# Splits of q, k, v at the front of odd slots, low parts on VectorE, and two PSUM banks by turns in a fused attention and two-layer feed-forward kernel

## The chip, the cores and the metric

One core of one Trainium2 chip. The time of a run is the device time in microseconds (us); lower is better. It is given as the median of several runs of the same program.

## The reference

Three stages, each fed by the one before, all in float32:

```python
def _attn_ref(q, k, v):                       # (8, 8, 576, 64) each, chunks of 64
    scores = scale * np.matmul(q_c, k_c.transpose(0, 1, 2, 4, 3))
    scores = scores - np.max(scores, axis=-1, keepdims=True)
    attn = np.exp(scores)
    attn = attn / (np.sum(attn, axis=-1, keepdims=True) + 1e-09)
    out = np.matmul(attn, v_c)
def _moe_ref(x, w_in, w_out):                 # 4608 x 512, 512 x 2048, 2048 x 512
    h = x @ w_in
    g = np.where(h > 0.0, h, np.exp(np.minimum(h, 0.0)) - 1.0)
    return g @ w_out
def _moe2_ref(x, w_gate, w_val, w_out):       # 512 x 1536, 1536 x 512
    return (1 / (1 + np.exp(-(x @ w_gate))) * (x @ w_val)) @ w_out
```

Attention is within chunks of 64 rows, so each head of each chunk is a small independent problem. The weights come as float64.

## The kernel before, in words

**Numbers in parts.** A float32 product is made of rounded parts. `split` (L94) writes the rounded (high) part of a tile as float32r, and a subtraction gives the rest (the low part). The products of the layers then take three passes, high by high, low by high, high by low (`PASSES`, L33). Scores and values of the later pairs use the parts too.

**Phase A and its slots.** The 4608 tokens form nine blocks of 512. For each block, layer 1 (512 to 2048) and layer 2 (2048 to 512) go over 16 strips of 128 hidden columns. One strip of one block is a slot `s`, and `slot` (L431) is an order written out by hand: scheduling is manual, so each engine takes its instructions in the order of the code, with waits where data or buffers ask for them. `layer_1(s)` makes 12 matmuls of 512 columns into a tile `h` (two buffers), `layer_2(s - 2)` makes 12 more into four tiles `y`. Between them ScalarE makes exp and relu (`elu_exp` L378, `elu_rest` L383), VectorE joins them one slot later (`elu_sum`, L386), and `elu_split` (L391) makes the high part on ScalarE and the low part on GpSimd.

**Attention inside the slots.** While block j goes through the layers, the attention of block j + 1 is made, one pair of groups for each two slots, 64 pairs in all. In an even slot pair `P` gets its scores (L243) and its softmax (`softmax_max` L281, `softmax_exp` L296, `softmax_sum` L299). In the next odd slot, pair `T` (the same one) is transposed (L306) and copied out of PSUM by ScalarE (`transposes_out`, L314). In the odd slot after that the pair, now called `V`, is multiplied by v (`values`, L337) and copied to the tile of x of the next block (`values_out`, L364). Pair `N` is the next one to be scored.

**Two kinds of pairs.** The first ten pairs of the slots (`P < P32`) use plain float32 matmuls. They fall in the first 20 slots. Before them `first_block` (L503) makes the attention of block 0. From pair 10 on, `split_qkv` (L230) makes high and low parts of q and v in one tile (`qv`: two ScalarE copies of 64 partitions, two VectorE subtractions) and of k in another (`kz`: a VectorE copy, a GpSimd subtraction). It stands late in the odd slot, after `transposes`. For these pairs `transposes_out` copies twice and issues two small DMAs (`tt`), which mirror the halves of the partitions, and `transposes_split` (L327) opens the next even slot with the high part of the probabilities on VectorE and the low part on GpSimd. `first_parts` (L275) lets ScalarE copy one half of a product out of PSUM, and VectorE adds the other (L292, L371).

**PSUM.** All of attention's matmuls in the slots use one tile of two banks, taken anew for each use (L209, L210); the pool has one buffer, so each new user waits until the last reader of the user before is done:

```python
            def ps_tile(name):
                return ps_a.tile([128, 2, 512], F32, tag="a", name=name)
```

**Other queues.** While slots 0 to 15 run, the weights of layers 1 and 2 are still being converted from float64: `convert` (L106) puts steps for ScalarE and VectorE into a list, and `bg(q[i])` takes some of them at four places in each slot. From slot 16 on to the end of attention that list is empty. In the last slot of a block `split_x` (L174) makes the parts of three chunks of the next block's x, and in the first slot of the next block the fourth; `y_out` (L419) copies the finished y out in the second and third slot, on ScalarE and VectorE by turns. SP issues all loads and stores in the order of the code; `load_raw(P + 1)` opens an even slot.

**Phase B.** After the last block of phase A come the gated layers 3 and 4. Attention plays no part in them.

Of the kernel before, what the change touches and what calls it, by code (L numbers as in the profile page):

```python
# [52 lines left out]
def kernel(  # L53
# [141 lines left out]
    def phase_a():  # L195
        with (
# [12 lines left out]
            def ps_tile(name):  # L209
                return ps_a.tile([128, 2, 512], F32, tag="a", name=name)  # L210
# [18 lines left out]

            def split_qkv(P):  # L230

                r = raws.pop(P)
                k = kz[P] = s_p[0].tile([128, 2, 2, 256], F32R, tag="kz", name="kz")
                t = qv[P] = s_p[0].tile([128, 2, 2, 256], F32R, tag="qv", name="qv", bufs=3)
                h0, h1 = halves
                nc.scalar.copy(out=t[h0, :, 0], in_=r[h0, :, 0:256])
                nc.scalar.copy(out=t[h1, :, 1], in_=r[h1, :, 0:256])
                nc.vector.tensor_copy(out=k[:, :, 0], in_=r[:, :, 256:512])  # L238
                nc.vector.tensor_sub(out=t[h1, :, 0], in0=r[h0, :, 0:256], in1=t[h0, :, 0])
                nc.vector.tensor_sub(out=t[h0, :, 1], in0=r[h1, :, 0:256], in1=t[h1, :, 1])  # L240
                nc.gpsimd.tensor_sub(out=k[:, :, 1], in0=r[:, :, 256:512], in1=k[:, :, 0])  # L241

            def scores(P):  # L243
                ps = st[P, "s"] = ps_tile("ps_s")
                if P < P32:
                    r = raws.pop(P)
                    for i in range(2):
                        for a in range(2):
                            nc.tensor.matmul(
                                out=ps[:, 0, (2 * i + a) * CH:(2 * i + a + 1) * CH],  # L250
                                lhsT=r[:, i, a * 128:(a + 1) * 128],
                                rhs=r[:, i, 256 + a * CH:256 + (a + 1) * CH],
                                start=True,
                                stop=True,
                            )
# [3 lines left out]
                k = kz.pop(P)  # L259
# [21 lines left out]
            def softmax_max(P):  # L281
# [3 lines left out]
                if P < P32:  # L285
                    ps = ps[:, 0, 0:256].rearrange("p (n k) -> p n k", n=4)
# [19 lines left out]
            def transposes(P):  # L306
                ps, p = ps_tile("ps_t"), st.pop((P, "p"))
                st[P, "tp"] = ps[:, 0, 0:256]
                for i in range(2):
                    nc.tensor.transpose(  # L310
                        ps[:, 0, 128 * i:128 * i + 128], p[:, 2 * i:2 * i + 2].rearrange("p n k -> p (n k)"), ident,
# [15 lines left out]
            def transposes_split(P):  # L327
# [6 lines left out]
                    nc.vector, nc.gpsimd,  # L334
                )

            def values(P):  # L337
                ps, t = ps_tile("ps_v"), st.pop((P, "t"))
                st[P, "v"] = ps
                if P < P32:  # L340
                    r = vals.pop(P)
                    for i in range(2):
                        for u in range(2):
                            nc.tensor.matmul(
                                out=ps[:, 0, 128 * i + u * CH:128 * i + (u + 1) * CH],
# [6 lines left out]
                    return  # L352
                for i in range(2):
# [10 lines left out]
            def values_out(P):  # L364
                ps, (x, o) = st.pop((P, "v")), place(P)
                if P < P32:
                    nc.scalar.copy(out=x[:, o:o + 256], in_=ps[:, 0, 0:256])
# [63 lines left out]
            def slot(s, steps=0):  # L431
# [12 lines left out]
                if even:  # L444
                    if is_pair(P + 1, P32):
                        load_raw(P + 1)
                    if is_pair(P - 1, P32):
                        transposes_split(P - 1)
# [17 lines left out]
                if not even and is_pair(V, P32):  # L466
                    values_out(V)
# [15 lines left out]
                if not even:  # L483
                    if is_pair(T):
                        transposes(T)
                    if is_pair(N, P32):
                        split_qkv(N)
                elu_exp(s)
                if even and is_pair(P):
                    softmax_sum(P)  # L490
                bg(q[2])
                if not even and is_pair(T):
                    transposes_out(T)
# [9 lines left out]
            def first_block(load_w):  # L503
# [28 lines left out]
                for k in range(len(pairs) + 5):  # L532
# [22 lines left out]
                    if (n := at(k - 4)) is not None:  # L555
                        ps = ps_v[n] = ps_tile("ps_v")[:, 0].rearrange("p (n u q) -> p n u q", n=4, u=2)
# [235 lines left out]
```

## Time and profile before

| | us |
|---|---|
| median of 3 runs | 1839.76 |
| lowest and highest run | 1838.08 and 1840.18 |
| profiled execution, its own time | 1839.62 |
| span of the profiled execution | 1837.8 |

| engine | share of the span busy |
|---|---|
| TensorE, matmuls | 98% |
| TensorE, weight loads | 81% |
| VectorE | 55% |
| ScalarE | 39% |
| GpSimd | 22% |

The span runs from the first to the last instruction; the rest of the execution's time lies around it. Times in the profile are counted from the start of the span. The engines are named PE (TensorE matmul), PEld (its weight loads), DVE (VectorE), ACT (ScalarE), POOL (GpSimd) and SP (the queue that issues DMAs). A row such as "a L92" is an instruction made at line 92 of the kernel that writes tile a; a line can be that of a helper, so tiles tell more. The ends of matmuls are modelled, so two matmuls that overlap in a row are one behind the other in truth.

### The profile page before, as it was taken

How to read it: one execution, taken by the hardware profiler on the slowest of the kernel's cores; microseconds unless marked ns; L12 is line 12 of the kernel's file. 1: busy time of each engine (PE TensorE's matmuls, PEld its weight loads, DVE VectorE, ACT ScalarE, POOL GpSimd, SP SyncE). 2: the span in 40 equal slices, each digit the busy share in tenths (PEclk: the TensorE clock that was granted, in tenths of full speed). 3: DMA queues.
4: the chain of work that ended last, by engine and by line, in shares of the span. 5: the costliest groups of instructions: out<-in, count | busy, mean ns of one | idle time of the engine just before them, and what ended most of it. 6: DMA issues, size and time to landing. Idle time of an engine off the chain costs nothing.

```text
span 1837.8 us, 21982 instructions
## 1 busy us (share of the span) xinstructions
PE 1798.4 (98%) x8176; PEld 1481.8 (81%) x8176; DVE 1014.6 (55%) x1671; ACT 724.9 (39%) x1411; POOL 412.8 (22%) x305
## 2 busy tenths in 40 slices
PE   7899999999999999999999999999999999999999
PEld 5778878788787878788888888888888888888887
DVE  6887887787888788876758622223222223132222
ACT  6666665566656566666754301111010101010100
POOL 2223454444444454543220000000000000000000
PEclk9899999999999999999999999999999999999999
DMA  6552121121212221212443100001010101010000
GB/s 215 179 170 94 48 76 53 54 81 46 78 58 66 58 72 53 75 60 82 157 121 122 61 18 23 24 1 46 1 46 1 46 1 46 0 47 0 24 1 23
DMA packets 49498, 111.52 MB, mean 61 GB/s; under 512 B 5872, under 2 KB 17904, under 8 KB 49392
## 3 DMA queue, kind: packets, MB, share of 16 engines
q1 hardware_dynamic: 49392, 110.12, 19.0%
q8 instruction: 65, 1.06, 0.2%
q14 instruction: 41, 0.34, 0.1%
HBM read 84.15 MB, written 18.87 MB: 56 GB/s over the span
## 4 chain that ended last, share of the span: by engine, by line
PE 83%; DVE 8%; ACT 5%; issue 2%; DMA 1%; SPq 0%; DVEq 0%; ACTq 0%
PE o L668 16%; PE pg L181 16%; PE pv L181 16%; PE h L181 16%; PE y L411 15%; PE ps_s L262 1%; DVE qv L240 1%; DVE kz L238 1%; PE ps_v L355 1%; DVE elu L387 1%; DMA tt<-tt 1%; DVE s L294 1%; ACT xs L90 1%; ACT elu L384 1%; DVE t L146 1%
## 5 line engine op out<-in xcount | busy, mean ns | idle before, releaser
L181 PE MATMUL h<-xs,w 128*128 128x512 f32 x1728 | 426.0, 395 | 1.3 <-DVE xs L96 1.3
L411 PE MATMUL y<-g,w 128*128 128x512 f32 x1728 | 424.0, 394 | 0.6 <-DVE y L428 0.6
L657 DVE TENSOR_TENSOR sg<-pv,sg 128x512 f32<-128x512 f32 x108 | 74.6, 691 | 549.8 <-PE pv L181 543.0
L411 PEld LDWEIGHTS y<-g,w 128*128 128x128 f32 x1728 | 319.7, 188 | 66.0 <-DVE y L428 1.0
L181 PEld LDWEIGHTS h<-xs,w 128*128 128x128 f32 x1728 | 317.8, 189 | 64.2 <-DVE xs L96 3.8
L652 ACT ACTIVATE sg<-pg 128x512 f32<-128x512 f32 x108 | 64.4, 597 | 673.5 <-PE pg L181 673.5
L181 PE MATMUL pg<-xs,w 128*128 128x512 f32 x1296 | 311.3, 389 | 0.0
L181 PE MATMUL pv<-xs,w 128*128 128x512 f32 x1296 | 311.3, 389 | 0.0
L668 PE MATMUL o<-w,g 128*128 128x512 f32 x1296 | 311.1, 389 | 0.0
L181 PEld LDWEIGHTS pv<-xs,w 128*128 128x128 f32 x1296 | 243.2, 188 | 50.5
L181 PEld LDWEIGHTS pg<-xs,w 128*128 128x128 f32 x1296 | 243.2, 188 | 50.5
L668 PEld LDWEIGHTS o<-w,g 128*128 128x128 f32 x1296 | 243.2, 188 | 50.5
L96 POOL TENSOR_TENSOR g<-elu,g 128x512 fp32r<-128x512 f32 x144 | 198.7, 1380 | 362.8 <-ACT g L90 353.9
L96 POOL TENSOR_TENSOR xs<-xr,xs 128x512 fp32r<-128x512 f32 x29 | 40.9, 1409 | 814.3 <-ACT xs L90 814.1
L387 DVE SCALAR_TENSOR_TENSOR elu<-h,elu 128x512 f32<-128x512 f32 x144 | 99.5, 691 | 44.6 <-ACT elu L384 42.9
L90 ACT CAST g<-elu 128x512 fp32r<-128x512 f32 x144 | 89.1, 618 | 51.3 <-DVE elu L387 50.4
L241 POOL TENSOR_TENSOR kz<-raw,kz 128x512 fp32r<-128x512 f32 x54 | 96.5, 1787 | 19.1 <-DVE kz L238 16.6
L381 ACT ACTIVATE elu<-h 128x512 f32<-128x512 f32 x144 | 86.0, 597 | 23.0 <-PE h L181 16.6
L96 POOL TENSOR_TENSOR pt<-tt,pt 128x512 fp32r<-128x512 f32 x54 | 70.0, 1297 | 104.9 <-DVE pt L92 98.6
L384 ACT ACTIVATE elu<-elu 128x512 f32<-128x512 f32 x144 | 91.0, 632 | 3.5
L240 DVE TENSOR_TENSOR qv<-raw,qv 64x512 fp32r<-64x512 f32 x54 | 90.3, 1672 | 1.7
L90 ACT CAST w<-t 128x512 fp32r<-128x512 f32 x68 | 42.2, 621 | 95.0 <-DVE t L146 93.8
(74 smaller groups left out, 1465.9 us busy)
## 6 DMA issues: line engine op xcount, KB each, us to landing
raw<-in_qkv SPq DMA_DIRECT2D x54, 512.0 KB, 3.6
wraw<-in_w_out SPq DMA_DIRECT2D x28, 512.0 KB, 3.6
xr<-ymid SPq DMA_DIRECT2D x36, 256.0 KB, 3.6
wraw<-in_w_in SPq DMA_DIRECT2D x16, 512.0 KB, 3.7
ymid<-y SPq DMA_DIRECT2D x32, 256.0 KB, 2.8
out<-o SPq DMA_DIRECT2D x32, 256.0 KB, 2.0
tt<-tt SPq DMA_DIRECT2D x108, 64.0 KB, 2.0
wraw<-in_w_gate SPq DMA_DIRECT2D x12, 512.0 KB, 3.5
```

The costliest lines, as they stand in the source:

```text
L90: nc.scalar.copy(out=out, in_=raw)
L96: lo_eng.tensor_sub(out=lo, in0=raw, in1=hi)
L181: nc.tensor.matmul(out=ps, lhsT=w[:, zw, kk * 128:(kk + 1) * 128], rhs=xs[key, kk][:, zx], start=(kk == 0 and n == 0), stop=(kk == KC - 1 ...
L240: nc.vector.tensor_sub(out=t[h0, :, 1], in0=r[h1, :, 0:256], in1=t[h1, :, 1])
L241: nc.gpsimd.tensor_sub(out=k[:, :, 1], in0=r[:, :, 256:512], in1=k[:, :, 0])
L381: nc.scalar.activation(out=e_t[s], in_=h_t[s], func=ACTF.Exp)
L384: nc.scalar.activation(out=e_t[s], in_=e_t[s], func=ACTF.Relu, scale=-1.0, bias=1.0)
L387: nc.vector.scalar_tensor_tensor(out=e_t[s], in0=h_t.pop(s), scalar=0.0, in1=e_t[s], op0=ALU.max, op1=ALU.subtract,)
L411: nc.tensor.matmul(out=y_t[j, e], lhsT=w[:, zw, e * 128:(e + 1) * 128], rhs=g[:, zx], start=(f == 0 and n == 0), stop=(f == F1 - 1 and n = ...
L652: nc.scalar.activation(out=sg, in_=pg, func=ACTF.Sigmoid)
L657: nc.vector.tensor_tensor(out=sg, in0=pv, in1=sg, op=ALU.mult)
L668: nc.tensor.matmul(out=o_t[t], lhsT=g[:, zx, t * 128:(t + 1) * 128], rhs=w[:, zw], start=(f == 0 and n == 0), stop=(f == F2 - 1 and n == 2),)
```

## The change

It has four parts.

- `split_qkv` is moved from behind `transposes` to the front of the odd slot, behind `elu_sum`. The high part of k becomes a function of its own, `split_k`, which stands before `values_out`; the rest stands behind `values_out`.
- The low part of k and the low part of the probabilities go from GpSimd to VectorE. `transposes_split` moves from the front of the even slot to behind `softmax_max`.
- The two banks are one tile for the whole phase. Plain float32 products and the transposes take one bank each, by turns (`bank`); the products of the later pairs take both.
- `transposes_out` stands right behind `elu_exp`, ahead of the third place of background steps.

```diff
--- before.py
+++ after.py
@@ -206,8 +206,14 @@
             s_p = [None]
             halves = (slice(0, 64), slice(64, 128))
 
-            def ps_tile(name):
-                return ps_a.tile([128, 2, 512], F32, tag="a", name=name)
+
+            banks = ps_a.tile([128, 2, 512], F32, name="banks")
+            turns = [0]
+
+            def bank(n):
+                turns[0] ^= 1
+                return banks[:, turns[0], 0:n]
+
 
             def load_raw(P):
                 if P < P32:
@@ -227,27 +233,29 @@
                 hp, c = divmod(i, 2)
                 return xr_tile(j + 1, hp), 256 * c
 
+
+            def split_k(P):
+                k = kz[P] = s_p[0].tile([128, 2, 2, 256], F32R, tag="kz", name="kz")
+                nc.vector.tensor_copy(out=k[:, :, 0], in_=raws[P][:, :, 256:512])
+
             def split_qkv(P):
-
-                r = raws.pop(P)
-                k = kz[P] = s_p[0].tile([128, 2, 2, 256], F32R, tag="kz", name="kz")
+                r, k = raws.pop(P), kz[P]
                 t = qv[P] = s_p[0].tile([128, 2, 2, 256], F32R, tag="qv", name="qv", bufs=3)
                 h0, h1 = halves
                 nc.scalar.copy(out=t[h0, :, 0], in_=r[h0, :, 0:256])
                 nc.scalar.copy(out=t[h1, :, 1], in_=r[h1, :, 0:256])
-                nc.vector.tensor_copy(out=k[:, :, 0], in_=r[:, :, 256:512])
+                nc.vector.tensor_sub(out=k[:, :, 1], in0=r[:, :, 256:512], in1=k[:, :, 0])
                 nc.vector.tensor_sub(out=t[h1, :, 0], in0=r[h0, :, 0:256], in1=t[h0, :, 0])
                 nc.vector.tensor_sub(out=t[h0, :, 1], in0=r[h1, :, 0:256], in1=t[h1, :, 1])
-                nc.gpsimd.tensor_sub(out=k[:, :, 1], in0=r[:, :, 256:512], in1=k[:, :, 0])
 
             def scores(P):
-                ps = st[P, "s"] = ps_tile("ps_s")
                 if P < P32:
-                    r = raws.pop(P)
+                    ps, r = bank(256), raws.pop(P)
+                    st[P, "s"] = ps
                     for i in range(2):
                         for a in range(2):
                             nc.tensor.matmul(
-                                out=ps[:, 0, (2 * i + a) * CH:(2 * i + a + 1) * CH],
+                                out=ps[:, (2 * i + a) * CH:(2 * i + a + 1) * CH],
                                 lhsT=r[:, i, a * 128:(a + 1) * 128],
                                 rhs=r[:, i, 256 + a * CH:256 + (a + 1) * CH],
                                 start=True,
@@ -256,7 +264,8 @@
                     if P + 1 < P32:
                         load_raw(P + 1)
                     return
-                k = kz.pop(P)
+                ps, k = banks, kz.pop(P)
+                st[P, "s"] = ps
                 for i in range(2):
                     for u in range(2):
                         nc.tensor.matmul(
@@ -283,7 +292,7 @@
                 m = a_p.tile([128, 4, 1], F32, tag="m", name="m")
                 ps = st.pop((P, "s"))
                 if P < P32:
-                    ps = ps[:, 0, 0:256].rearrange("p (n k) -> p n k", n=4)
+                    ps = ps.rearrange("p (n k) -> p n k", n=4)
                     nc.vector.tensor_reduce(out=m[:, :, 0], in_=ps, op=ALU.max, axis=AX.X)
                     nc.vector.tensor_tensor(out=s, in0=ps, in1=m.to_broadcast([128, 4, CH]), op=ALU.subtract)
                     return
@@ -304,11 +313,11 @@
                 nc.vector.tensor_tensor(out=p, in0=e4[:, :, 0:CH], in1=d.to_broadcast([128, 4, CH]), op=ALU.mult)
 
             def transposes(P):
-                ps, p = ps_tile("ps_t"), st.pop((P, "p"))
-                st[P, "tp"] = ps[:, 0, 0:256]
+                ps, p = bank(256), st.pop((P, "p"))
+                st[P, "tp"] = ps
                 for i in range(2):
                     nc.tensor.transpose(
-                        ps[:, 0, 128 * i:128 * i + 128], p[:, 2 * i:2 * i + 2].rearrange("p n k -> p (n k)"), ident,
+                        ps[:, 128 * i:128 * i + 128], p[:, 2 * i:2 * i + 2].rearrange("p n k -> p (n k)"), ident,
                     )
 
             def transposes_out(P):
@@ -331,18 +340,18 @@
                     tt.rearrange("p u i q -> p (u i) q"),
                     t[:, :, :, 0].rearrange("p u i q -> p (u i) q"),
                     t[:, :, :, 1].rearrange("p u i q -> p (u i) q"),
-                    nc.vector, nc.gpsimd,
+                    nc.vector, nc.vector,
                 )
 
             def values(P):
-                ps, t = ps_tile("ps_v"), st.pop((P, "t"))
-                st[P, "v"] = ps
+                t = st.pop((P, "t"))
                 if P < P32:
-                    r = vals.pop(P)
+                    ps, r = bank(256), vals.pop(P)
+                    st[P, "v"] = ps
                     for i in range(2):
                         for u in range(2):
                             nc.tensor.matmul(
-                                out=ps[:, 0, 128 * i + u * CH:128 * i + (u + 1) * CH],
+                                out=ps[:, 128 * i + u * CH:128 * i + (u + 1) * CH],
                                 lhsT=r[:, i, u * 128:(u + 1) * 128],
                                 rhs=t[:, 128 * i + u * CH:128 * i + (u + 1) * CH],
                                 start=True,
@@ -350,6 +359,7 @@
                             )
                     load_values(P + 1)
                     return
+                ps = st[P, "v"] = banks
                 for i in range(2):
                     for u in range(2):
                         nc.tensor.matmul(
@@ -364,7 +374,7 @@
             def values_out(P):
                 ps, (x, o) = st.pop((P, "v")), place(P)
                 if P < P32:
-                    nc.scalar.copy(out=x[:, o:o + 256], in_=ps[:, 0, 0:256])
+                    nc.scalar.copy(out=x[:, o:o + 256], in_=ps)
                     return
                 x1 = st.pop((P, "v1"))
                 for a, p in enumerate(halves):
@@ -444,8 +454,6 @@
                 if even:
                     if is_pair(P + 1, P32):
                         load_raw(P + 1)
-                    if is_pair(P - 1, P32):
-                        transposes_split(P - 1)
                     if is_pair(P):
                         scores(P)
                     if is_pair(P, P32):
@@ -463,8 +471,15 @@
                     elu_sum(s - 1)
                 if even and is_pair(P):
                     softmax_max(P)
-                if not even and is_pair(V, P32):
-                    values_out(V)
+                if even and is_pair(P - 1, P32):
+                    transposes_split(P - 1)
+                if not even:
+                    if is_pair(N, P32):
+                        split_k(N)
+                    if is_pair(V, P32):
+                        values_out(V)
+                    if is_pair(N, P32):
+                        split_qkv(N)
                 bg(q[0])
                 if s >= EARLY:
                     layer_1(s, 2)
@@ -480,17 +495,14 @@
                     softmax_exp(P)
                 if last:
                     split_x(nxt, 1, nc.vector)
-                if not even:
-                    if is_pair(T):
-                        transposes(T)
-                    if is_pair(N, P32):
-                        split_qkv(N)
+                if not even and is_pair(T):
+                    transposes(T)
                 elu_exp(s)
+                if not even and is_pair(T):
+                    transposes_out(T)
                 if even and is_pair(P):
                     softmax_sum(P)
                 bg(q[2])
-                if not even and is_pair(T):
-                    transposes_out(T)
                 elu_rest(s)
                 if last:
                     split_x(nxt, 2, nc.gpsimd)
@@ -553,7 +565,7 @@
                                 ps[:, i], work[n][2][:, 2 * i:2 * i + 2].rearrange("p v k -> p (v k)"), ident,
                             )
                     if (n := at(k - 4)) is not None:
-                        ps = ps_v[n] = ps_tile("ps_v")[:, 0].rearrange("p (n u q) -> p n u q", n=4, u=2)
+                        ps = ps_v[n] = bank(512).rearrange("p (n u q) -> p n u q", n=4, u=2)
                         for i in range(2):
                             nc.tensor.matmul(
                                 out=ps[:, 2 * i:2 * i + 2].rearrange("p v a q -> p (v a q)"),
```

## Rows read from the trace of the kernel before

**Rows 1.** The page: busy time by engine, and one group of instructions

```profile
PE 1798.4 (98%) x8176; PEld 1481.8 (81%) x8176; DVE 1014.6 (55%) x1671; ACT 724.9 (39%) x1411; POOL 412.8 (22%) x305
...
L90 ACT CAST g<-elu 128x512 fp32r<-128x512 f32 x144 | 89.1, 618 | 51.3 <-DVE elu L387 50.4
```

**Rows 2.** Stretches: busy us and count by engine, granted TensorE clock, DMA share, GB/s

```profile
40.00:150.00 110.00, 97.38 (x471) 79.70 (x469) 91.44 (x188) 77.05 (x150) 24.44 (x14) 0.94 0.52 161
...
250.00:860.00 610.00, 598.07 (x2801) 487.87 (x2800) 484.17 (x738) 372.70 (x758) 294.03 (x206) 1.00 0.21 62
860.00:1838.00 978.00, 974.04 (x4298) 806.20 (x4296) 337.32 (x570) 189.62 (x325) 38.22 (x28) 1.00 0.13 41
```

**Rows 3.** Waits of 44 to 157 us: total us, times, longest

```profile
ACT w L90 <- DVE t L146: 33.0, 21, 2.9
PE ps_s L249 <- ACT t L319: 12.0, 7, 3.8
...
DVE m L287 <- PE ps_s L249: 1.8, 3, 0.8
```

**Rows 4.** Timeline at 54 us: start, us, instruction, [idle before <-releaser]

```profile
54.58 1.97 PE L249 MATMUL ps_s<-raw 128*128 128x64 f32 x8 [3.83 <-ACT t L319]
```

**Rows 5.** Timeline of one pair of slots inside a block

```profile
611.12 0.63 PE L262 MATMUL ps_s<-kz,qv 128*128 128x256 f32 x4
...
611.59 2.90 PE L181 MATMUL h<-xs,w 128*128 128x512 f32 x12
611.79 0.75 ACT L279 COPY s<-ps_s 64x256 f32<-64x256 f32 x2 [1.57 <-PE ps_s L262]
611.87 0.43 DVE L92 CAST pt<-tt 128x512 fp32r<-128x512 f32 x1 [0.82 <-DMA tt<-tt]
...
612.43 1.30 POOL L96 TENSOR_TENSOR pt<-tt,pt 128x512 fp32r<-128x512 f32 x1 [1.93 <-DVE pt L92]
612.94 0.85 DVE L292 TENSOR_TENSOR s<-ps_s,s 64x256 f32<-64x256 f32 x2
...
613.81 1.29 POOL L96 TENSOR_TENSOR g<-elu,g 128x512 fp32r<-128x512 f32 x1
613.82 0.42 DVE L293 TENSOR_REDUCE m<-s 128x4 f32<-128x256 f32 x1
...
614.27 1.10 DVE L294 TENSOR_TENSOR s<-s,m 128x256 f32<-128x256 f32 x1
...
617.05 0.63 PE L355 MATMUL ps_v<-pt,qv 128*128 128x256 f32 x4
...
619.39 1.38 DVE L238 CAST kz<-raw 128x512 fp32r<-128x512 f32 x1
...
620.79 0.69 DVE L239 TENSOR_TENSOR qv<-raw,qv 64x512 fp32r<-64x512 f32 x1
620.84 1.80 POOL L241 TENSOR_TENSOR kz<-raw,kz 128x512 fp32r<-128x512 f32 x1 [0.36 <-DVE kz L238]
...
621.51 1.68 DVE L240 TENSOR_TENSOR qv<-raw,qv 64x512 fp32r<-64x512 f32 x1
...
623.24 0.63 PE L262 MATMUL ps_s<-kz,qv 128*128 128x256 f32 x4
```

**Rows 6.** Waits of 250 to 860 us

```profile
PE ps_s L262 <- POOL kz L241: 7.3, 14, 1.0
```

**Rows 7.** Timeline of TensorE: first scores of the third and of the eighth block

```profile
255.84 0.39 PE L262 MATMUL ps_s<-kz,qv 128*128 128x256 f32 x1 [0.97 <-POOL kz L241]
...
761.15 0.39 PE L262 MATMUL ps_s<-kz,qv 128*128 128x256 f32 x1 [0.97 <-POOL kz L241]
```

**Rows 8.** Timeline of the first and third slot of one block

```profile
461.79 1.22 DVE L96 TENSOR_TENSOR xs<-xr,xs 128x512 fp32r<-128x512 f32 x1 [0.70 <-ACT xs L90]
...
476.69 2.89 PE L411 MATMUL y<-g,w 128*128 128x512 f32 x12
...
477.48 0.69 DVE L428 COPY y<-y 128x512 f32<-128x512 f32 x1 [0.60 <-DMA ymid<-y]
```

## The prediction, made before the changed kernel was run

> **What bounds the kernel now.** I read the page's busy times first, then the stretches, then the waits, then the order of work in one pair of slots. TensorE is busy for 98% of the span [rows 1], so only its waits can be won. Three stretches differ [rows 2]. From 860 us on TensorE is busy for 974.04 of 978 us, a matmul each 0.227 us (978 / 4298), and the change does not touch that code. In 250:860 it loses some 12 of 610 us, in 40:150 some 12.6 of 110. Busy time flatters TensorE, since matmul ends are modelled; below I go by starts.
>
> The first slots lose to one wait: seven times, 12.0 us in all, `scores` waits for ScalarE's copy of the transposes (L319) [rows 3]. Its single PSUM tile is still to be read by that copy: at 54.58 TensorE had sat for 3.83 us [rows 4]. The copy is late because ScalarE stands in the weight conversion: it waits 33.0 us there for VectorE's sums, and VectorE waits only 1.8 us for TensorE's scores [rows 3]. These two set their own pace; TensorE is held to it.
>
> The attention stage has a pair of slots with no wait: scores at 611.12, values at 617.05, next scores at 623.24, a period of 12.12 us [rows 5]. Eight pairs, a block, would be 97.0 us. But from the scores at 255.84 to those at 761.15, five blocks, 505.3 us pass [rows 7], so a block loses 4.1 us against 97.0. Most of it stands at the block's edge, where the splits of x join the queues and `scores` waits for GpSimd's low part of k, 14 times [rows 6]. With the sixth edge the stage loses some 6 x 4.1 = 24.6 us.
>
> **The change, part by part.** Times in this part are after the scores' first matmul of a pair (611.12 is 0, values 5.93, next scores 12.12) [rows 5].
>
> *Low part of k to VectorE.* GpSimd loses 1.80 us a pair. VectorE gains one subtraction of 512 elements: 0.69, as L239 when it runs clear. But L240, the same work beside GpSimd's L241, took 1.68, and the conversion L238 beside GpSimd's low part of g 1.38 [rows 5]; the like conversion L92, clear, took 0.43. So VectorE gives 0.69 and gets back about 1.0 twice. Bounds: 0.69 if clear, 1.68 if held.
>
> *Splits at the front of odd slots.* VectorE now does elu_sum (0.69, taken as L239's, as long), the high part of k (0.43), `values_out`, then three subtractions. I lay it out: values at 5.93, elu_sum to 6.7, high k to 7.1, `values_out` (ScalarE's copies, 0.67 after the values as after the scores, end at 7.35) to 8.2, low k to 8.9, first q to 9.7. ScalarE has put its two q copies (0.62 each, as the high part of g [rows 1]: 7.35 to 8.6) ahead of that high part, so GpSimd's low part of g (1.29) runs 9.7 to 10.9 and holds the last subtraction, which ends at 11.4. The next scores load weights one matmul, 0.23, before 12.12, at 11.9: 0.5 to spare, where before L240 ended (623.19) just under the scores (623.24) [rows 5]. High g comes 1.2 later, but layer 2 wants it only behind the next scores and 12 matmuls of layer 1, at 12.12 + 0.47 + 2.72 = 15.3 (0.47 is from 611.12 to 611.59 [rows 5], 2.72 is 12 x 0.227); free. If that cover went, it would cost those 1.2. No DMA moves but those of `transposes_out`, two per odd slot on SP; it now stands ahead of a background step, of which this stage has none. In the first slots it has no DMA. SP's load of the next k, q, v is released earlier, as the raw tile is read out sooner; nothing.
>
> *Low part of the probabilities to VectorE, after `softmax_max`.* GpSimd loses 1.30 a pair. In even slots VectorE no longer begins with the conversion L92 that waits for a DMA. elu_sum runs before the scores; the two sums L292 (0.85, after the ScalarE copies that end at 1.42) to 2.3, the maximum (0.42) to 2.75; the subtraction L294 is held by GpSimd's g, about 2.1 to 3.4, and ends 0.3 after it, 3.7 (before: 615.37, 0.27 after GpSimd). Then high 0.43 and low 0.69: 4.85. The values load weights at 5.7: 0.85 to spare, so in a pair in the middle of a block nothing is won and nothing lost. `softmax_sum` ends near 5.95, and the transposes want it at about 9.1.
>
> *At a block's edge* the parts collide anew. The splits of k and q end before the scores, by the order above with GpSimd's x parts between, at about -0.5: the wait at the scores goes. But in the first slot VectorE has the low part of x chunk 3 (1.22 held [rows 8], 0.7 clear) and that of chunk 1 ahead of elu_sum, which ends near 3.5. ScalarE's high g (0.62) and GpSimd's 1.29 follow, to 5.55, L294 ends at 5.85, the probabilities at 7.0: the values wait 7.0 - 5.7 = 1.3 us. That is late next. In the slot after, the chain shifts by as much and the last q part ends some 0.2 late. Two slots on, VectorE's copy of y (477.48, 0.69) now follows the two parts of the probabilities, 1.12, where it followed one, 0.43. It ended at 478.17, and TensorE overwrote that tile at 476.69 + 9 x 0.227 = 478.73 [rows 8]: 0.56 to spare, less 0.7 and the shift; I take 0.35. New loss 1.85 a block against 4.1: 2.25 won, six times, **13.5 us**. Bounds: 0 if the edge gives all back, 24.6 if nothing takes its place.
>
> *Two banks by turns.* Scores, values and transposes are three uses a pair, so each finds the other bank than the one before it; scores no longer follow the transposes' copy. At most 12.0 us, plus 0.7 for transposes behind `values_out`. But the pace of VectorE and ScalarE stays: what TensorE wins is lead, until another need holds it: the transposes want the probabilities of the slot before, layer 2 its g. That is most of a slot, 6 to 7 us. VectorE has light slots once conversion ends and can catch up, so the lead is kept. I take **6 us**; bounds 1.8 (only VectorE's wait for TensorE goes) and 12.7.
>
> **Sum.** The profiled execution took 1839.62, within 0.2 of the runs' median 1839.76. 1839.6 - 13.5 - 6 = 1820.
>
> **Rivals.** *The queue of VectorE becomes the bound (slower).* The probabilities are ready 0.85 before the values need them; if VectorE's low part were held by GpSimd once more (1.29), they would be 0.44 late in each of the 54 pairs, 24 us, against 19.5 won: 1844. It decides at 0.36 late a pair. For it: VectorE is busy 484 of 610 us and GpSimd 294 there [rows 2], and work goes to the busier. Against: GpSimd keeps one operation a slot, and that one is already charged. The Trainium skill, "Perfetto Trace Analysis", section "Optimizing Scalar/DVE Operations", speaks for this rival: a saturated VectorE may hand work to GpSimd, and moving work between those two might not help, since they share a read port. By it the two moves would win nothing and only the banks would pay, 1834; the trace shows VectorE held by GpSimd (1.68 against 0.69), which bears out the shared port, but not a saturated VectorE.
>
> *The edge gives everything back.* Waits of the values and of y replace those of the scores in full: 1839.6 - 6 = 1834. For it: the 1.3 above is my least certain step.
>
> *The edge closes wholly and the first slots gain all:* 1839.6 - 24.6 - 12.7 = 1802. Against: VectorE's pace [rows 3].
>
> *The banks do not part.* `banks` is one tile; if a wait covers the tile and not the bank, scores wait as before: 1839.6 - 13.5 = 1826. In the trace nothing shows which.
>
> **How the numbers follow.** Forecast 0.50, edge gives back 0.22, all closes 0.12, banks do not part 0.08, slower 0.08. The range, 1807 to 1835, leaves out the slower case, most of the case where all closes, and ends of the bounds. About 0.2% (3.7 us) is what a measurement of this kernel can tell from no change. Below 1836: nearly all of the forecast, most of the edge case, and the two others, 0.86; within: 0.05; above 1843.5: 0.09.
>
> **What would show it.** The row "scores waits for ScalarE t L319" gone, and TensorE's waits for GpSimd's kz with it; block periods near 98.9 instead of 101; a wait of the values for VectorE's pt, about 1.3 us, once a block; pairs still 12.12; L240's time nearer 0.7 for one of the two q parts. I am wrong if pairs inside a block are longer than 12.12, if scores in the first slots still wait, or if the first slots win 12 us.

## The result, and the profile after

| | median us | runs from ... to |
|---|---|---|
| before | 1839.97 | 1838.08 to 1840.64 |
| changed | 1822.46 | 1821.61 to 1823.99 |

The ratio is 0.9907, with an interval of 0.9890 to 0.9925: 0.9% faster, more than the interval leaves open, and 2.5 us from the 1820 forecast. The profiled execution took 1822.07 us. The two terms of the sum came out unlike their sizes, though, and that their errors nearly cancelled is luck.

The page of the changed kernel: busy time by engine.

```profile
PE 1787.4 (98%) x8176; PEld 1480.7 (81%) x8176; DVE 1012.6 (56%) x1779; ACT 729.6 (40%) x1411; POOL 260.2 (14%) x197
```

GpSimd lost 152.6 us of work against [rows 1], and VectorE, which took it, is busy no longer than before.

The stretches (columns as in [rows 2]):

```profile
40.00:150.00 110.00, 99.13 (x475) 80.78 (x474) 91.92 (x189) 77.19 (x151) 24.50 (x14) 0.94 0.52 161
250.00:860.00 610.00, 604.96 (x2875) 502.18 (x2874) 497.40 (x854) 389.68 (x781) 165.23 (x114) 1.00 0.23 69
```

In 250:860 TensorE went from 598.07 to 604.96 us, in 40:150 only from 97.38 to 99.13. The attention stage itself is read from one header of the timeline of the scores of pairs 10 to 63: start of the first and the last of 216 matmuls, before and after.

```profile
L262 PE MATMUL ps_s<-kz,qv x216: 278/280/388, 169.3 to 837.0; 128*128 128x256 f32 x108
```

```profile
L271 PE MATMUL banks<-kz,qv x216: 278/279/282, 168.5 to 819.4; 128*128 128x256 f32 x108
```

The stage took 667.7 us and takes 650.9: **16.8 us won** there. The first slots gave only 169.3 - 168.5 = **0.8 us**. Together 17.6; the two profiled executions differ by 1839.62 - 1822.07 = 17.55. The 0.8 us show no gain: five kernels below (splits late, low k on GpSimd, both runs on the parts of the probabilities, `elu_sum` first) have the changed kernel's code in the slots up to 15, and in their profiled executions pair 10 starts between 170.0 and 171.5. From the third pair's scores to those of pair 10, 169.33 - 54.58 = 114.75 us passed before and 168.53 - 53.94 = 114.59 after: the first slots won nothing that shows.

The first slots' waits, 44 to 157 us, against [rows 3]:

```profile
ACT w L90 <- DVE t L146: 32.1, 21, 2.5
...
PE banks L257 <- ACT t L328: 9.0, 7, 2.9
DVE d L310 <- ACT e L306: 8.4, 7, 1.7
```

The wait that the banks by turns were to end is still there, seven times: the scores (now L257) wait for ScalarE's copy of the transposes (now L328), which lies in the other bank. TensorE's waits in 165 to 860 us, by contrast, are down to a single kind, six times, once a block (matmuls, then weight loads):

```profile
PE banks L365 <- DVE pt L96: 5.0, 6, 0.9
```

```profile
PEld banks L365 <- DVE pt L96: 7.6, 6, 1.3
```

The first slot of one block after the change, the timeline of 540 to 562 us:

```profile
545.81 1.48 POOL L96 TENSOR_TENSOR xs<-xr,xs 128x512 fp32r<-128x512 f32 x1 [5.93 <-ACT xs L90]
...
546.16 1.67 DVE L249 TENSOR_TENSOR qv<-raw,qv 64x512 fp32r<-64x512 f32 x1
...
548.59 0.63 PE L271 MATMUL banks<-kz,qv 128*128 128x256 f32 x4
...
550.67 0.69 DVE L96 TENSOR_TENSOR xs<-xr,xs 128x512 fp32r<-128x512 f32 x1 [1.13 <-ACT xs L90]
551.40 0.69 DVE L397 SCALAR_TENSOR_TENSOR elu<-h,elu 128x512 f32<-128x512 f32 x1
...
552.87 1.28 POOL L96 TENSOR_TENSOR g<-elu,g 128x512 fp32r<-128x512 f32 x1 [2.17 <-ACT g L90]
...
553.34 1.09 DVE L303 TENSOR_TENSOR s<-s,m 128x256 f32<-128x256 f32 x1
554.36 0.41 DVE L92 CAST pt<-tt 128x512 fp32r<-128x512 f32 x1
554.81 0.69 DVE L96 TENSOR_TENSOR pt<-tt,pt 128x512 fp32r<-128x512 f32 x1
555.55 0.74 PE L365 MATMUL banks<-pt,qv 128*128 128x256 f32 x4 [0.82 <-DVE pt L96]
```

The last part of q ends at 547.83, 0.76 ahead of the scores, which wait for nothing. Then VectorE idles for a part of x with `elu_sum` behind it, and the chain elu_sum, high g, low g on GpSimd, subtraction, parts of the probabilities ends at 555.50, 6.91 after the scores. The values are late by it. The stage's first pair lasts 12.60 us (12.59 before), a block's first pair 13.24 to 13.31, every other 12.12 to 12.16.

### The profile page after: what moved, and what is told of

Its sections match the earlier page's. It is cut to its first block, busy times and chain, and to the rows that moved or that the text cites. A ratio compares the mean times of both kernels' runs of the same rounds, so it can differ in the third digit from the quotient of the medians.

```text
span 1820.3 us, 21691 instructions
## 1 busy us (share of the span) xinstructions
PE 1787.4 (98%) x8176; PEld 1480.7 (81%) x8176; DVE 1012.6 (56%) x1779; ACT 729.6 (40%) x1411; POOL 260.2 (14%) x197
## 4 chain that ended last, share of the span: by engine, by line
PE 91%; DVE 4%; ACT 3%; issue 1%; DMA 0%; SPq 0%; DVEq 0%; ACTq 0%
PE y L421 19%; PE h L181 19%; PE o L680 16%; PE pv L181 16%; PE pg L181 16%; PE banks L365 1%; PE banks L271 1%; PE banks L319 1%; DVE t L146 1%; DVE elu L397 1%; ACT t L124 1%; ACT w L90 1%; DMA qkv<-in_qkv 0%; DVE t L140 0%; ACT g L90 0%
## 5 line engine op out<-in xcount | busy, mean ns | idle before, releaser
L96 POOL TENSOR_TENSOR g<-elu,g 128x512 fp32r<-128x512 f32 x144 | 213.0, 1479 | 606.8 <-ACT g L90 348.9
L288 ACT COPY s<-banks 64x256 f32<-64x256 f32 x216 | 79.1, 366 | 122.9 <-PE banks L271 71.5
L301 DVE TENSOR_TENSOR s<-banks,s 64x256 f32<-64x256 f32 x108 | 45.5, 422 | 62.7 <-ACT s L288 62.0
```

The source lines that it names most:

```text
L96: lo_eng.tensor_sub(out=lo, in0=raw, in1=hi)
L288: nc.scalar.copy(out=t[p], in_=parts_of(st[P, what], p, a)[0])
```

## The experiments

All changes are against the changed kernel unless another is named. "Stage" is the time between the first and the last scores of pairs 10 to 63, read as above (667.7 before, 650.9 changed).

### Turns: one tile, two tiles, and the copy's place

**No turns.** The tile is taken anew for each use, as before, and nobody alternates.

```diff
-            banks = ps_a.tile([128, 2, 512], F32, name="banks")
-            turns = [0]
+            def ps_tile():
+                return ps_a.tile([128, 2, 512], F32, tag="a", name="banks")
             def bank(n):
-                turns[0] ^= 1
-                return banks[:, turns[0], 0:n]
+                return ps_tile()[:, 0, 0:n]
...
```

> The changed kernel without turns: each product takes the one tile of two banks anew, as before the change. Theory 1, the turns never parted anything, since a wait covers the tile: same waits in the first slots, total 1822 within 1.5. Theory 2, the turns are worth something in the first block or where a use needs only one bank: scores' waits for ScalarE's t go from 9.0 back to 12.0 us and the total to 1824 to 1826.

Measured: 1822.75 us, ratio 0.9903 (0.9888 to 0.9918). Its waits of 44 to 157 us:

```profile
PE banks L256 <- ACT t L327: 9.0, 7, 2.9
```

Time and wait are those of the changed kernel, to 0.3 us and to the digit, as theory 1 said. The turns inside one tile part nothing.

**Two tiles.** In slots 0 to 15 the banks are two tiles of one bank each; from slot 16 on one tile of two banks.

```diff
...
             def bank(n):
                 turns[0] ^= 1
-                return banks[:, turns[0], 0:n]
+                return both[0][:, turns[0], 0:n] if s_p[0] else both[turns[0]][:, 0:n]
...
+                both[:] = [ps_1.tile([128, 512], F32, name=f"bank{i}") for i in range(2)]
...
+                s_p[0], both[:] = p2, [ps_a.tile([128, 2, 512], F32, name="banks")]
```

> The changed kernel, with the two banks as two tiles of their own while slots 0 to 15 run (one tile of both banks from slot 16 on, as now). Theory 1, a wait covers the whole tile, not the bank: scores' seven waits for ScalarE's copy of the transposes (9.0 us) and the transposes' four for the copy of the values (2.1) go from TensorE's rows; TensorE wins lead, some 5 to 8 us, total 1815 to 1818. Theory 2, the banks part already and what holds the first slots is the pace of VectorE and ScalarE: the waits get other names, the total stays at 1822 within 2.

Measured: 1821.22 us, ratio 0.9900 (0.9885 to 0.9915). The timeline at slots 14, 16 and 18 (at 136.24, 153.23 and 168.00), first of this kernel, then of the changed one:

```profile
136.24 1.10 PE L255 MATMUL bank<-raw 128*128 128x64 f32 x8
...
153.23 1.10 PE L255 MATMUL banks<-raw 128*128 128x64 f32 x8 [1.78 <-ACT t L326]
154.15 4.59 PE L181 MATMUL h<-xs,w 128*128 128x512 f32 x12
154.77 1.57 DVE L96 TENSOR_TENSOR xs<-xr,xs 128x512 fp32r<-128x512 f32 x1 [1.35 <-ACT xs L90]
...
168.00 0.63 PE L269 MATMUL banks<-kz,qv 128*128 128x256 f32 x4
```

```profile
141.86 1.10 PE L257 MATMUL banks<-raw 128*128 128x64 f32 x8 [0.89 <-ACT t L328]
...
155.52 1.00 PE L257 MATMUL banks<-raw 128*128 128x64 f32 x8
```

The scores wait for the copy no more but once, where the tile of two banks begins (153.23), and at slot 14 TensorE leads by 141.86 - 136.24 = 5.6 us. At slot 16 the lead is 2.3, at slot 18 (168.5 against 168.00) 0.5, less than executions differ by. So two tiles do part the uses, and a lead as large as the forecast's 6 us arises; but it is lost again where the weight conversion ends. There block 1's first layer takes 4.59 instead of some 3.0, as it needs the parts of x, which stand in ScalarE's and VectorE's queues behind the last conversions: one is still in the making at 154.77. The time is therefore that of theory 2, 1822 within 2, though its reason, that the banks parted already, is not so. In 44 to 157 us TensorE's waits have other names: the transposes wait 2.8 us for the probabilities and layer 2 waits 2.6 us for low parts of g, as the prediction said that lead would be held.

**The copy late.** Only `transposes_out` goes back behind the third place of background steps.

```diff
-                if not even and is_pair(T):
-                    transposes_out(T)
                 if even and is_pair(P):
                     softmax_sum(P)
                 bg(q[2])
+                if not even and is_pair(T):
+                    transposes_out(T)
```

> The changed kernel with its copy of the transposes put back behind the third place of background steps. Theory 1 (that place is what shortened the scores' waits for the copy from 12.0 to 9.0 us): the waits of 44 to 157 us are back at 11 to 13 us, the attention stage keeps its 98.2 us a block, 1823.5 to 1826 us. Theory 2 (the copy's early place also matters in the attention stage, where its two DMAs feed the parts of the probabilities): blocks grow beyond 99 us and the time is above 1828.

Measured: 1824.77 us, ratio 0.9917 (0.9903 to 0.9932); the stage as in the changed kernel (170.7 to 821.7, 651.0). The waits of 44 to 157 us:

```profile
PE banks L257 <- ACT t L328: 11.0, 6, 3.9
```

This is as theory 1 said: the copy's place made most of the fall from 12.0 to 9.0. In time it is worth some 2 us, which the intervals do not part from nothing.

### The attention stage: place or engine

**Splits late again**, with all low parts still on VectorE.

```diff
-                if not even:
-                    if is_pair(N, P32):
-                        split_k(N)
-                    if is_pair(V, P32):
-                        values_out(V)
-                    if is_pair(N, P32):
-                        split_qkv(N)
+                if not even and is_pair(V, P32):
+                    values_out(V)
...
                     transposes(T)
+                if not even and is_pair(N, P32):
+                    split_k(N)
+                    split_qkv(N)
                 elu_exp(s)
```

> The changed kernel, with the splits of q, k, v back behind the transposes, low parts still on VectorE. Theory 1 (place): the chain ends 0.9 us after the scores want it at the edge, scores wait there for VectorE's qv, a block loses 2.5 to 3 us where it now loses 1.2, total 1830 to 1834. Theory 2 (engine): the total stays within 3 us of 1822.

Measured: 1842.36 us, ratio 1.0011 (1.0002 to 1.0021): more than the whole gain is gone, and more than was expected to go. The stage took 669.5. TensorE's waits of 165 to 860 us:

```profile
PE banks L271 <- DVE qv L249: 7.7, 6, 1.3
PE banks L271 <- DVE qv L248: 4.0, 6, 0.7
PE banks L365 <- DVE pt L96: 2.6, 3, 0.9
```

The scores wait for the splits again, now for VectorE instead of GpSimd [rows 6]. The splits late with low k on GpSimd, as before the change, were not run, so the 20 us are the price of the late place with low k on VectorE.

**Low k on GpSimd**, at the new place: one word, `nc.vector` to `nc.gpsimd`, in `split_qkv`.

> The changed kernel, with the low part of k back on GpSimd at its new, early place. Theory 1, the place in the queues is what won the edge: pairs inside a block stay at 12.13 and blocks lose at most 0.5 more, total 1822 to 1826. Theory 2, freeing GpSimd is what won it (GpSimd's own 1.8 us and the VectorE subtraction that it holds): scores wait for GpSimd's kz at every edge as before, block periods near 101, total 1835 to 1838.

Measured: 1823.49 us, ratio 0.9912 (0.9897 to 0.9927), no difference from the changed kernel that these intervals show; the stage took 650.8 (170.5 to 821.3). VectorE's groups of 250 to 760 us, in this kernel:

```profile
L249 DVE TENSOR_TENSOR qv<-raw,qv 64x512 fp32r<-64x512 f32 x42 | 39.7, 945 | 1.3
L248 DVE TENSOR_TENSOR qv<-raw,qv 64x512 fp32r<-64x512 f32 x42 | 34.8, 829 | 1.3
```

and in the changed one:

```profile
L249 DVE TENSOR_TENSOR qv<-raw,qv 64x512 fp32r<-64x512 f32 x42 | 70.3, 1674 | 1.3
L247 DVE TENSOR_TENSOR kz<-raw,kz 128x512 fp32r<-128x512 f32 x42 | 29.1, 693 | 1.3
L248 DVE TENSOR_TENSOR qv<-raw,qv 64x512 fp32r<-64x512 f32 x42 | 28.8, 685 | 1.3
```

VectorE spends 0.693 + 0.685 + 1.674 = 3.05 us a pair on the three subtractions, against 0.829 + 0.945 = 1.77 on two: the move costs it 1.28 us a pair, all of it hidden. At the new place k's engine makes no difference that shows, as theory 1 said.

**Parts of the probabilities at the front of the even slot again**, both on VectorE.

```diff
                         load_raw(P + 1)
+                    if is_pair(P - 1, P32):
+                        transposes_split(P - 1)
                     if is_pair(P):
                         scores(P)
...
-                if even and is_pair(P - 1, P32):
-                    transposes_split(P - 1)
```

> The changed kernel, with the parts of the probabilities back at the front of the even slot, both on VectorE. Theory 1, their new place behind softmax_max is what makes the values wait at the edge: that wait (1.1 us a block) goes, but x chunk 3 and elu_sum now stand behind them, so layer 1 waits 0.5 to 1 us there: total 1818 to 1822, pairs inside a block 12.13. Theory 2, VectorE's conversion that waits for the DMA costs in every pair, as everything on VectorE stands behind it: pairs inside a block over 12.2, total 1826 or more.

Measured: 1839.90 us, ratio 0.9997 (0.9987 to 1.0007): the whole gain is gone; the stage took 668.4. VectorE's timeline in a pair inside a block:

```profile
611.68 0.43 DVE L92 CAST pt<-tt 128x512 fp32r<-128x512 f32 x1 [2.12 <-DMA tt<-tt]
...
612.87 0.69 DVE L397 SCALAR_TENSOR_TENSOR elu<-h,elu 128x512 f32<-128x512 f32 x1
```

VectorE stands 2.12 us for the mirroring DMA with `elu_sum` behind it. TensorE's waits of 165 to 860 us show what comes late by that: the transposes, y and the scores.

```profile
PE banks L319 <- ACT qv L246: 5.6, 11, 0.9
PE y L421 <- DVE y L438: 4.2, 4, 1.9
PE banks L271 <- DVE qv L249: 2.7, 4, 0.8
```

The values' wait is gone, as theory 1 said, but the time is on theory 2's side: beside 14.0 to 14.5 us for a block's first pair, several other pairs now take 12.3 to 14.3. The place behind `softmax_max` is therefore as necessary as that of the splits: without either, the whole gain is lost.

**Low part of the probabilities on GpSimd**, at the new place: the last argument of `transposes_split` from `nc.vector` to `nc.gpsimd`.

> The changed kernel, with the low part of the probabilities back on GpSimd at the new place. Theory 1 (VectorE's 0.69 against GpSimd's 1.3): ready 0.65 later, so the values wait 1.75 at the edge instead of 1.1, and pairs inside a block just make it (0.15 to spare): total 1825 to 1828. Theory 2, GpSimd's freedom matters: the low part also holds VectorE's softmax sums and the values wait in every pair, total over 1835.

Measured: 1829.44 us, ratio 0.9938 (0.9923 to 0.9953): 7 us of the gain lost, of which 5.2 in the stage, which took 656.1. TensorE's waits of 165 to 860 us:

```profile
PE banks L365 <- POOL pt L96: 4.8, 6, 0.8
PE banks L319 <- ACT qv L246: 3.5, 6, 0.6
```

The time is 1.4 us above theory 1's range, and the values' wait did not grow as that theory said: 4.8 us against 5.0. The loss stands in the two pairs behind that one, with 12.77 to 12.97 and up to 12.37 us, where the transposes now wait. ScalarE's timeline in the first of them:

```profile
573.91 0.60 ACT L391 ACTIVATE elu<-h 128x512 f32<-128x512 f32 x1 [2.48 <-POOL g L96]
```

GpSimd makes the low part of the probabilities ahead of the low part of g, which so ends later; ScalarE's next exp waits 2.48 us for it (1.45 in the changed kernel), with the copies of the values behind it in the queue. That the transposes come late by this is read from the order, not tested.

Here the engine counts. The Trainium skill, "Perfetto Trace Analysis", section "Optimizing Scalar/DVE Operations", warns that moving work between VectorE and GpSimd might not help, as they share a read port. The trace agrees for k (no change shown) and not for the probabilities (7 us), where another operation stood behind the moved one in GpSimd's queue and ScalarE waited for it.

### The rest of the edge

**`elu_sum` first.** In a block's first slot VectorE waits for a part of x with `elu_sum` behind it (550.67 above). The two change places.

```diff
-                if f == 0 and j > 0:
-                    split_x(j, KC - 1, nc.vector)
                 if s > 0:
                     elu_sum(s - 1)
+                if f == 0 and j > 0:
+                    split_x(j, KC - 1, nc.vector)
```

> The changed kernel, with elu_sum ahead of the low part of x chunk 3 in the first slot of a block (two lines of code change places). Theory 1, the values wait at the edge because VectorE sits idle for ScalarE's chunk 3 with elu_sum queued behind it, and GpSimd's low part of g then holds the softmax subtraction: the wait goes, block periods fall from 98.2 to about 97.1, six or seven times 1.1, total 1815 to 1816. Theory 2, VectorE has simply too much work at the edge: the loss moves to the next scores or to y, block periods stay near 98, total 1821 to 1823.

Measured: 1817.67 us, ratio 0.9880 (0.9865 to 0.9895). The stage took 644.7 (170.9 to 815.6), 6.2 less, some 1.0 for each of six edges. The values' wait is gone, so the chain does begin with the idle time before 550.67. The total is 1.7 us above theory 1's range; pair 10 came at 170.9 in this execution.

**Both**, two tiles and `elu_sum` first.

> Two tiles for the banks in slots 0 to 15 and elu_sum ahead of x chunk 3. The first won 1 us and the second 5. Theory 1, they lie in different stretches and add: 1816 to 1817. Theory 2, TensorE's lead is lost where the parts of x for block 1 are late at slot 16; with elu_sum ahead of chunk 3 that is the place that moves, so more of the lead is kept: 1812 to 1815.

Measured: 1814.83 us, ratio 0.9859 (0.9844 to 0.9873). The stage takes 644.2, and pair 10 starts at 168.2. The time lies in theory 2's range, but its reason is not shown: against the kernel with `elu_sum` first alone (170.9) pair 10 comes 2.7 us earlier, no more than executions differ by, and TensorE's lead over the changed kernel still falls from 5.5 us at slot 14 (136.38) to 0.3.

### What holds the first slots

ScalarE's and VectorE's timelines in that last kernel, with two tiles and `elu_sum` first:

```profile
100.88 0.62 ACT L90 CAST w<-t 128x512 fp32r<-128x512 f32 x1 [2.13 <-DVE t L146]
...
102.47 0.41 ACT L304 ACTIVATE e<-s 128x256 f32<-128x256 f32 x1
```

```profile
100.76 0.42 DVE L137 TENSOR_SCALAR t<-t 128x512 uint32<-128x512 uint32 x1
102.92 0.43 DVE L308 TENSOR_REDUCE d<-e 128x4 f32<-128x260 f32 x1 [1.74 <-ACT e L304]
```

ScalarE's high copy of a converted weight waits 2.13 us for VectorE's sum, and the exponentials stand behind it; then VectorE waits 1.74 us for the exponentials. Each waits for the other in turn. So, in that kernel, the copy is issued later, at the next place of background steps.

```diff
+    high = {}
     def bg(n):
+        for m in list(high):
+            high.pop(m)()
...
             load(n + ahead)
+            high[n] = lambda: make_high(n)
+
+        def make_high(n):
             w = halves[n] = tiles[n][2].tile([128, 2, 512], F32R, tag="w", name="w")
             copy(nc.scalar, w[:, 0], parts[n].bitcast(F32))
         def rest(n):
+            high.pop(n, bool)()
```

> Two tiles and elu_sum first, as in the kernel of 1814.8 us; besides, ScalarE's high copy of a converted weight, which waits for VectorE's sum, is issued at the next place of background steps rather than right behind that sum's issue. Theory 1 (ScalarE's queue order sets the first slots: the exponentials and elu stand behind a copy that waits for VectorE): the 33 us that ScalarE waits for VectorE's sums fall below half, VectorE's wait for the exponentials (8.4 us) falls below 4, block 1's slots come 3 to 8 us earlier, 1807 to 1812 us. Theory 2 (VectorE's own work sets the end of the conversion, so that the lead is lost at slot 16 whatever ScalarE does): the waits move, slot 16 stands where it did within 1 us, 1813 to 1816 us.

Measured: **1803.83 us**, ratio 0.9801 (0.9783 to 0.9818), 36 us below the kernel before, the fastest of all and 3 us below theory 1's range. Waits of 44 to 157 us, and the scores of pair 10 in TensorE's timeline:

```profile
ACT w L90 <- DVE t L150: 21.2, 20, 1.8
...
DVE d L316 <- ACT e L312: 3.0, 4, 1.1
```

```profile
157.01 0.63 PE L277 MATMUL banks<-kz,qv 128*128 128x256 f32 x4
```

Pair 10 comes 11.2 us earlier than at 168.2, where 3 to 8 were expected, and from 65 us on a pair of first slots takes 13.0 to 13.1 with no wait of TensorE's matmuls. ScalarE's wait fell by a third, not by half as expected, VectorE's wait for the exponentials from 8.4 to 3.0, as expected.

**The same with one tile:**

> The same as the run with the high copies issued later, but with the one tile of the changed kernel (turns inside one tile). Theory 1 (the wait of the scores for ScalarE's copy of the transposes comes of ScalarE standing in the conversion): with ScalarE free, that copy comes early, the wait of 9.0 us falls below 4, and the time is within 1.5 us of the run with two tiles. Theory 2 (the tile itself holds the scores): the wait stays above 6 us and the time is 1816 to 1819, as with elu_sum first alone.

Measured: 1807.05 us, ratio 0.9819 (0.9803 to 0.9834). The wait for the copy is 3.5 us, twice. Theory 1 holds for the wait (3.5, below 4); two tiles still bring 3.2 us more, not the 1.5 expected at most, with intervals that overlap.

**The kernel before, with nothing but the later copies:**

> The kernel before, with ScalarE's high copies of converted weights issued at the next place of background steps and nothing else. Theory 1 (the order of ScalarE's queue alone sets the first slots, with no need of two tiles or of any part of the change): the scores' waits of 12.0 us fall below 5, the scores of pair 10 come 8 to 11 us earlier than 169.3, 1828 to 1832 us. Theory 2 (it works only together with the copy of the transposes ahead of the background steps): waits stay above 8 us, less than 4 us is won, 1836 or more.

Measured: 1832.56 us, ratio 0.9961 (0.9948 to 0.9975), half a microsecond outside the range of theory 1. Pair 10 starts at 161.6 instead of 169.3, the stage lasts 667.7 as before, and the scores' waits of 44 to 157 us fell from 12.0 to 4.4. The order of ScalarE's queue alone gives 7 us, without any part of the change.

## Why the prediction came right, point by point

**The edge: right in mechanism, undersized.** The prediction had the scores' wait go, and the values wait 1.3 us for the low part of the probabilities once a block. Both stand in the rows: weight loads wait 1.3 us, six times, and the probabilities are ready 6.91 after the scores, where it said 7.0. The two smaller terms, 0.2 at the next scores and 0.35 at y, have no row: no wait of TensorE but that of the values is left. The stage's 53 intervals at 12.13 make 642.9; 650.9 less 0.3 within the last scores leaves 7.7 lost: 0.5 in the stage's first pair and 1.1 to 1.2 at each of six edges, in place of 1.85; a block takes 98.2, where it said 98.9. The loss before, by the same working, is 24.5, where the prediction took 24.6. With the 16.8 us measured in place of 13.5, this term was 3.3 short, by the new loss alone.

**Pairs inside a block: right.** They last 12.13, and one part of q takes 0.69, the other 1.67.

**"VectorE gives 0.69 and gets back about 1.0 twice": wrong, without effect.** The conversion of k went from 1.38 [rows 5] to 0.42 on average, but by its place: it is 0.42 with low k on GpSimd as well, and 1.41 with the splits late. The last part of q gave nothing back: 1.67 as before. Slack of VectorE covered it, as the prediction's own layout of the odd slot allowed, which did not use this gain: it had the last subtraction held and 0.7 us ahead of the scores (11.4 of 12.12), and it ends 0.76 ahead.

**"Two banks by turns: I take 6 us": the step that failed.** The rival *the banks do not part* was the true case, with a chance of 0.08: one tile is waited for as a whole. It gave 1826, and 1823 with the measured 16.8 for the edge. The wait fell from 12.0 to 9.0, mostly by the copy's place, to which the prediction gave no price in the first slots; the time from the third pair to pair 10 fell by 0.2, which shows no gain. And the reason given for 6 us, "VectorE has light slots once conversion ends and can catch up, so the lead is kept", fails too: with two tiles the lead was there at slot 14 and gone at slot 18.

**"VectorE and ScalarE set their own pace": half right.** They did hold TensorE, but the pace was made by one copy's place in ScalarE's queue, not by their work; with that copy later, the same work let the first slots run free. The prediction's own condition, "I am wrong if scores in the first slots still wait", is met: the total held by luck, as a term 3.3 short met one 5.2 too long.

**The slower rival** did not occur: no pair inside a block grew. Its premise, that the parts of the probabilities on VectorE would be held by GpSimd, is not in the rows; 0.69 is their mean too.

## What to carry to other kernels

At the front of an in-order queue an operation that waits costs everything behind it; ask for each waiting instruction what stands behind it and whether another engine waits for that in turn, for moving one copy was worth as much here as whole parts of the change. Turning between banks pays only if the program's waits tell the banks apart, so give each its own tile and look for the wait in the trace. A lead won at one wait is kept only if the next thing that must be on time, here block 1's parts of x, is early as well.

## What the runs showed of the hardware

**Two waits of TensorE came with half the clock.** In the changed kernel the scores at 53.94 follow two idle times, 2.88 and 2.78 us (TensorE's timeline):

```profile
45.02 1.31 PE L257 MATMUL banks<-raw 128*128 128x64 f32 x8 [2.88 <-ACT t L328]
...
53.94 1.97 PE L257 MATMUL banks<-raw 128*128 128x64 f32 x8 [2.78 <-ACT t L328]
55.66 4.75 PE L181 MATMUL h<-xs,w 128*128 128x512 f32 x12
...
69.66 1.00 PE L257 MATMUL banks<-raw 128*128 128x64 f32 x8
70.48 2.98 PE L181 MATMUL h<-xs,w 128*128 128x512 f32 x12
```

and the stretches around them (granted clock third from the end):

```profile
53.90:57.00 3.10, 3.06 (x11) 2.87 (x12) 2.35 (x6) 2.72 (x5) 2.05 (x1) 0.50 0.77 227
...
60.30:63.00 2.70, 2.70 (x14) 2.20 (x13) 2.30 (x6) 1.86 (x4) 1.29 (x1) 1.00 0.45 178
```

The granted clock was 1.00 in 42 to 45 us, 0.69 in 45 to 47, 0.50, the 1.2 GHz level, from 47 to 59, and 1.00 again from 60.3 on. Scores and layer 1 so take 0.97 + 1.77 = 2.7 us longer than at 69.66. The prediction charged nothing for it, though [rows 4] showed the same 1.97.

**A VectorE subtraction was held by GpSimd's.** A subtraction of two SBUF tiles takes VectorE 0.69 us alone (554.81 above) and 1.67 beside one of GpSimd's: at 546.16 it begins while GpSimd makes a low part of x, until 547.29, and ends 0.54 behind that. The Trainium skill, "SBUF — State Buffer", section "Who interferes with whom", says that a VectorE instruction with two inputs in SBUF contends with a reading GpSimd instruction, and that the order of issue decides who blocks the other; the trace agrees, with a mean of 1674 ns over 42 such parts. What "gets back about 1.0 twice" did not expect is that taking GpSimd's low k away did not shorten that part but lengthened it, from 945 to 1674 ns: it then stood beside GpSimd's next operation.
